# q and k as scaled fp16 pairs in the score matmuls of a bucketed attention with a spectral mixer

## The chip, the core and the metric

One core of a Trainium2 chip runs the whole program. The metric is device time in microseconds, as the median over several runs of the same program; the lower the better.

## The reference

Attention comes first, in 4 batches × 8 heads of 768 tokens with 64 numbers each. Each token of q and k gets a bucket out of 6 signs of a projection, and a query sees only keys of its own bucket. Then each batch goes through a mixer.

```python
q_bits = einsum('bhsd,dk->bhsk', q, proj) > 0        # the same for k; 6 bits make a bucket
mask = q_bucket[:, :, :, None] == k_bucket[:, :, None, :]
scores = where(mask, q @ k.T / sqrt(64), -1e9)
attn = exp(scores - max(scores)); attn = attn / (sum(attn) + 1e-9)
x = (attn @ v), heads side by side                    # 4 x 768 x 512
theta = x @ w_theta
y = w_tok_r @ (x * cos(theta)) + w_tok_i @ (x * sin(theta))
u = x + y
out = u + maximum(u @ w_ch, 0)
```

The weights of the mixer are float64 (read as two 32-bit words each); q, k, v and proj are float32.

## The kernel before

**Precision.** TensorE multiplies pairs: each float32 operand is split into a high part, rounded to the type of the matmul, and a low part, the rest. In the scores the type is fp32r, fp32 data that TensorE takes in one pass; in P·V and the token mixing it is fp16.

**Heads come in pairs.** For each of 16 pairs (4 batches × 4), `prep_qk` loads q and k of two heads as `raw` (128 partitions: head and dimension; 768 tokens), makes `hl` (high by ACT or DVE, L569 and L571; low = raw − high by POOL or DVE, L575), and takes the bucket signs by a small matmul `pb` (L597). `assemble` then copies, per head, parts of `hl` and the sign rows into `qt` and `kt` by ten DMAs. `qt` and `kt` exist three times, and hold two score operands side by side: half 0 of 108 rows (64 high, 32 of the low part, 12 bucket signs with a weight of ±2^40) and half 1 of 97 rows (64 high, 32 low, one row for the maximum). The signs with the large weight push scores of other buckets far down.

**Maxima.** For each head `maxima` (L695 and after) multiplies half 0 of `qt` by half 0 of `kt` into `sq` in 9 units and reduces each on DVE to a row maximum `mc`; PE transposes it (`pmx`), DVE makes a row of it, and a DMA puts the row into half 1 of `qt` (L719 in `put`). The row goes through the second score matmul, with −1 in `kt`, and so subtracts the maximum.

**Chunks.** `step` computes P·V in chunks of 512 columns, 18 for a pair and 288 in all. A chunk is: 2 or 4 score matmuls into a PSUM bank `st` (there are two such banks, the pool s); ACT's exp of it into `pf` (L773); a copy rounded to fp16, `p`, by ACT (L779); the rest `pf − p` by POOL (L785); and 12 matmuls `po` into a bank of the head. Three products (p1·v1, p1·v2, p2·v1) make a P·V. V has been split into an fp16 pair `vv`, scaled by a power of two (`prep_v`: largest magnitude by DVE, two small matmuls `pa` and three DVE steps, L459 to L473 and L351 to L353).

**Mixer.** After each batch `moe` transposes x (`pt_x`), multiplies by w_theta (`ps_th`), takes sine and cosine on ACT, mixes tokens (`py`, 864 matmuls of 512 fp16 columns), and multiplies by w_ch (`ps_r`). The weights are unpacked and split during the first batch (`wf_t`, `wf_th`, `wf_ch`, `pwt`, `wtk`).

**The order.** All these pieces are recorded as operations with a priority, the engines that may run them with assumed durations, and the buffers that they use. A planner (`issue_all`) walks simulated time and gives each free engine the ready operation of least priority, looks at buffers, and lets operations with two possible engines go where there is room. So the order of all engines follows from the numbers at the end of the file: the priorities count chunks (`G`, step of a pair, plus offsets such as `QK0`, `MX0`, `PF`). The instructions then run in this order on each engine, with waits between engines. DMAs are all issued from the queue of SP, one after another. Every matmul is written in the helper `mm` (L75), so PE rows carry that line and are told apart by their tiles.

Of the kernel before, what the change touches and what calls it, by code (L numbers as in the profile page):

```python
# [31 lines left out]
def lsh_attention_moe_kernel(ctx: ExitStack, tc: tile.TileContext, q, k, v, proj, w_theta, w_tok_r, w_tok_i, w_ch, aff, out):  # L32
# [412 lines left out]
    def prep_v(b, hp, prio):  # L445
# [11 lines left out]
        def amax():  # L457
            t["am"] = ap_.tile([P, 1], F32, tag="am" + svb.tag, bufs=1, name=f"vam_{b}_{hp}")
            DVE.tensor_reduce(t["am"], src(), AX.XY, ALU.max, apply_absolute_value=True)  # L459
# [21 lines left out]
        def high():  # L481
            t["vv"] = ap_.tile([P, 2, T, W2], F16, tag=sv.tag, bufs=1, name=f"vv_{b}_{hp}")
            t["vf"] = vf = t["vv"].rearrange("p h t w -> p (h t) w")
            ACT.activation(vf[:, :, :D], src(), AF.Copy, scale=sc)

        def ones():
# [666 lines left out]
```

## Time and profile before

| | |
|---|---|
| median of 3 runs | 830.68 us (830.67 to 832.88) |
| profiled execution | 829.88 us, its span 827.8 us |
| PE, PEld | 768.0 us, 532.5 us busy |
| DVE, ACT, POOL | 562.5, 519.4, 497.8 us busy |
| DMA | 77.88 MB on the queue of SP, mean 95 GB/s |

PE is TensorE's matmul, PEld its weight load, which overlaps PE; DVE is VectorE, ACT ScalarE, POOL GpSimd, SP the engine that issues DMAs. In a group of instructions, "out<-in" are tiles, "xN" is a count, and after the bar stand busy us, mean ns of one, and the idle time before them with what ended it. Matmuls overlap in the pipeline, so the distance from start to start tells their cost, not the mean duration. In a table of stretches the numbers after the length are busy us on PE, PEld, DVE, ACT and POOL, then the granted clock of TensorE (1.00 is full), the share of the DMA engines and GB/s.

### The profile page before, as it was taken

Reading aid. Unit: us, or ns where it says so; the run is one execution under the profiler, and the core shown is the slowest. Engines: PE = TensorE matmul, PEld = TensorE weight load, DVE = VectorE, ACT = ScalarE, POOL = GpSimd, SP = SyncE. Lnnn points to the kernel's source line nnn. Section 1 sums busy time; section 2 is a strip of 40 time slices with the busy share of each in tenths; the row PEclk is TensorE's granted clock in tenths of the full one; section 3 lists DMA queues with packets and bytes.
Section 4 is the critical chain, followed back from the end, with each engine's and each line's share of the span. In section 5 each row is a group of like instructions: output and inputs, shape, how many; then the busy total and the mean of one; then the engine's idle time right before and its main releaser. Section 6 shows DMA issues by size and latency. Waiting matters only on the chain. (4 is left out here: it accounts for less than half of the span.)

```text
span 827.8 us, 17652 instructions
## 1 busy us (share of the span) xinstructions
PE 768.0 (93%) x6744; PEld 532.5 (64%) x6744; DVE 562.5 (68%) x940; ACT 519.4 (63%) x889; POOL 497.8 (60%) x506
## 2 busy tenths in 40 slices
PE   3788898889999999899899999999899999999998
PEld 1466676667655677668657666777657667675456
DVE  7988799897877756775986455675986454336323
ACT  4476798788884625787886455567886454557201
POOL 3386799887684727794868455573878463541200
PEclk9978899899999999999999999999999999999999
DMA  8566564744034334452243432542243330000001
GB/s 232 139 213 172 148 190 122 178 129 100 30 84 116 92 105 119 114 141 65 58 100 95 112 92 51 122 101 70 61 100 94 75 72 18 15 14 1 1 1 76
DMA packets 35267, 78.99 MB, mean 95 GB/s; under 512 B 7264, under 2 KB 13040, under 8 KB 35184
## 3 DMA queue, kind: packets, MB, share of 16 engines
q1 hardware_dynamic: 35184, 77.88, 36.2%
q8 instruction: 53, 0.87, 0.4%
q14 instruction: 30, 0.25, 0.1%
HBM read 32.51 MB, written 6.29 MB: 47 GB/s over the span
## 5 line engine op out<-in xcount | busy, mean ns | idle before, releaser
L785 POOL TENSOR_TENSOR p<-pf,p 128x512 f16<-128x512 f32 x288 | 361.5, 1279 | 174.6 <-ACT p L779 131.4
L773 ACT ACTIVATE pf<-st 128x512 f32<-128x512 f32 x288 | 164.5, 593 | 125.8 <-PE st L75 98.7
L695 DVE TENSOR_REDUCE mc<-sq 128x1 f32<-128x512 f32 (+1 forms) x288 | 191.8, 684 | 61.6 <-PE sq L75 59.8
L75 PE MATMUL py<-z,wtk 128*128 128x512 f16 x864 | 217.1, 380 | 0.3 <-POOL z L963 0.2
L75 PE MATMUL st<-qt,kt 108*128 108x512 f32 (+3 forms) x768 | 198.5, 373 | 13.8 <-ACT pf L773 13.4
L779 ACT ACTIVATE p<-pf 128x512 f16<-128x512 f32 x288 | 172.1, 629 | 14.8 <-PE po L75 12.1
L75 PEld LDWEIGHTS <-p 128*128 128x128 f16 x3456 | 134.5, 100 | 38.7 <-issue 17.3
L75 PE MATMUL po<-vv,p 128*128 128x65 f16 (+1 forms) x3456 | 156.8, 196 | 1.7 <-POOL p L785 1.1
L75 PE MATMUL sq<-kt,qt 108*128 108x512 f32 (+1 forms) x384 | 132.2, 408 | 24.1 <-DVE mc L695 13.7
L75 PEld LDWEIGHTS st<-qt,kt 108*128 108x128 f32 (+1 forms) x768 | 121.6, 195 | 38.7 <-ACT pf L773 25.6
L75 PEld LDWEIGHTS <-wtk 128*128 128x128 f16 x864 | 72.4, 98 | 82.7 <-issue 21.2
L75 PEld LDWEIGHTS sq<-kt,qt 108*128 108x128 f32 x384 | 69.2, 200 | 53.9 <-DVE mc L695 29.7
L963 POOL TENSOR_TENSOR z<-f,z 128x512 f16<-128x512 f32 x38 | 50.9, 1350 | 62.0 <-ACT z L957 48.7
L75 PE MATMUL ps_th<-wth,h_x 128*128 128x512 f32 x192 | 62.1, 405 | 2.2 <-DVE z L918 1.3
L952 DVE SCALAR_TENSOR_TENSOR f<-x,zsc,z 128x512 f32<-128x512 f32 x48 | 56.8, 1226 | 9.4 <-ACT z L940 7.1
L75 PE MATMUL ps_r<-wch,h_u 128*128 128x512 f32 x192 | 62.7, 407 | 0.0
L879 ACT ACTIVATE h_u<-pt_u 128x512 fp32r<-128x512 f32 x24 | 14.3, 596 | 61.5 <-PE pt_u L874 55.3
L998 DVE SCALAR_TENSOR_TENSOR x<-ps_r,x 128x512 f32<-128x512 f32 x24 | 16.6, 691 | 49.0 <-PE ps_r L75 49.0
L75 PEld LDWEIGHTS ps_th<-wth,h_x 128*128 128x128 f32 x192 | 34.9, 188 | 11.4 <-DVE z L918 1.8
L75 PEld LDWEIGHTS ps_r<-wch,h_u 128*128 128x128 f32 x192 | 34.8, 189 | 9.9 <-DVE l_u L883 1.1
L991 DVE SCALAR_TENSOR_TENSOR x<-py,sw,x 128x512 f32<-128x512 f32 x24 | 17.8, 743 | 32.8 <-PE py L75 32.8
L75 PE MATMUL ps_th<-wth,l_x 128*128 128x512 f32 x96 | 38.4, 400 | 0.1
(123 smaller groups left out, 889.7 us busy)
## 6 DMA issues: line engine op xcount, KB each, us to landing
qt<-hl SPq DMA_DIRECT2D x31, 384.0 KB
kt<-hl SPq DMA_DIRECT2D x31, 384.0 KB
raw<-in_q_dram SPq DMA_DIRECT2D x16, 384.0 KB
raw<-in_k_dram SPq DMA_DIRECT2D x16, 384.0 KB
vb<-in_v_dram SPq DMA_DIRECT2D x16, 384.0 KB
out_dram<-x SPq DMA_DIRECT2D x24, 256.0 KB
qt<-hl SPq DMA_DIRECT2D x62, 96.0 KB
kt<-hl SPq DMA_DIRECT2D x62, 96.0 KB
```

Of the source, the lines that this page charges most:

```text
L75: PE.matmul(out_, l, r, start=start, stop=stop, skip_group_check=True)
L695: DVE.tensor_reduce(col()[:, cs], u["sq"], AX.X, ALU.max)
L773: ACT.activation(wide("pf", spf, F32), u["st"], AF.Exp, scale=1.0 / math.sqrt(D))
L779: ACT.activation(o_, u["pf"], AF.Copy)
L785: return lambda: eng.tensor_tensor(wide("p2", sp2, F16), u["pf"], u["p1"], ALU.subtract)
L879: ACT.activation(u["hi"], u["pt"], AF.Copy)
L952: DVE.scalar_tensor_tensor(u["f"], tl[b][:, tt], zsc[:, b : b + 1], t["zw"][r][:, tt], ALU.mult, ALU.mult)
L963: return lambda: eng.tensor_tensor(t["z"][r, 1][:, tt], u["f"], t["z"][r, 0][:, tt], ALU.subtract)
L991: DVE.scalar_tensor_tensor(tl[b][:, to], res["py"], t["sw"][:, to : to + 1], tl[b][:, to], ALU.mult, ALU.add)
L998: DVE.scalar_tensor_tensor(tl[b][:, to], r_["ps"], 0.0, tl[b][:, to], ALU.max, ALU.add)
```

## The change

- `hl`, `qt`, `kt` and the rows of signs and maxima are fp16 instead of fp32r. q and k of a pair are each scaled by a power of two before the split. The counts and shapes of score matmuls stay; a weight load of `kt` or `qt` is now an instruction of its own in the program, as it was for `p`.
- The scale comes from a sum of squares: ACT squares `raw` with a running sum (`accum_out`), a matmul with a tile of ones adds the partitions, and DVE makes scales and the inverse scale in seven steps on columns (`root_scale` and `scale`). High is `raw × scale`, low is `raw × scale − high`, always on DVE.
- exp takes the inverse scale of the pair as a per-partition operand, and log(4096) as a bias column, where it had constants.
- For V the same sum of squares takes the place of the largest magnitude: one ACT instruction, one matmul and four DVE steps.
- `hl` has two buffers instead of one. Bucket weight and limits are smaller, to fit fp16.
- The planner's durations for scores and first copies and some 40 of its numbers are others. The duration that it assumes for exp (490 ns) is the same.

```diff
-    FREE = dict(ft=2, mc=2, hl=1, rows=1, nat=2, vv=2, x=2, z0=1, z1=1, xt=2, **BUFS)
+    FREE = dict(ft=2, mc=2, hl=2, rows=1, sc=3, nat=2, vv=2, x=2, z0=1, z1=1, xt=2, **BUFS)
...
+    def root_scale(total, r, inv):
+        DVE.tensor_scalar(r, total, 1e-30, None, ALU.max)
+        DVE.tensor_scalar(r.bitcast(U32), r.bitcast(U32), 24, 23, ALU.logical_shift_right, ALU.logical_shift_left)
+        DVE.tensor_scalar(inv, r, 2.0**66, None, ALU.mult)
+        DVE.tensor_scalar(r.bitcast(U32), inv.bitcast(U32), MASK, None, ALU.bitwise_xor)
...
-            DVE.tensor_reduce(t["am"], src(), AX.XY, ALU.max, apply_absolute_value=True)
+            ACT.activation(t["vf"][:, :, W1 : W1 + D], src(), AF.Square, scale=2.0**-14, accum_out=t["ss"])
+        def total():
+            t["pa"] = bank(sa, [P, 1], f"pa_{b}_{hp}")
+            mm(t["pa"], ones, t["ss"], True, True)
...
-    qts = [ap_.tile([P, 2, S], F32R, tag=f"qt{j}", bufs=1, name=f"qt{j}") for j in range(SETS)]
-    kts = [ap_.tile([P, 2, S], F32R, tag=f"kt{j}", bufs=1, name=f"kt{j}") for j in range(SETS)]
+    qts = [ap_.tile([P, 2, S], F16, tag=f"qt{j}", bufs=1, name=f"qt{j}") for j in range(SETS)]
+    kts = [ap_.tile([P, 2, S], F16, tag=f"kt{j}", bufs=1, name=f"kt{j}") for j in range(SETS)]
...
+                    ACT.activation(t["hl"][:, 1, i], t["raw", i], AF.Square, scale=1.0 / RAISE, accum_out=t["sc"][:, i : i + 1])
...
-                            ACT.activation(t["hl"][:, 0, i], t["raw", i], AF.Copy)
+                            ACT.activation(t["hl"][:, 0, i], t["raw", i], AF.Copy, scale=t["sc"][:, 2 + i : 3 + i])
-                            DVE.tensor_copy(t["hl"][:, 0, i], t["raw", i])
+                            DVE.tensor_scalar(t["hl"][:, 0, i], t["raw", i], t["sc"][:, 2 + i : 3 + i], None, ALU.mult)
-                    return lambda: eng.tensor_tensor(t["hl"][:, 1, i], t["raw", i], t["hl"][:, 0, i].bitcast(F32), ALU.subtract)
+                    DVE.scalar_tensor_tensor(t["hl"][:, 1, i], t["raw", i], t["sc"][:, 2 + i : 3 + i], t["hl"][:, 0, i], ALU.mult, ALU.subtract)
...
+        def scale():
+            c = [t["sc"][:, n : n + 1] for n in range(7)]
+            root_scale(t["pa"], t["sc"][:, 2:4], t["sc"][:, 4:6])
+            DVE.scalar_tensor_tensor(c[3], c[4], SPAN / 2, c[3], ALU.mult, ALU.min)
+            DVE.scalar_tensor_tensor(c[5], c[2], 2 / SPAN, c[5], ALU.mult, ALU.max)
+            DVE.scalar_tensor_tensor(c[6], c[4], 0.25 / math.sqrt(D), c[5], ALU.mult, ALU.mult)
...
-                    ACT.activation(wide("pf", spf, F32), u["st"], AF.Exp, scale=1.0 / math.sqrt(D))
+                    ACT.activation(wide("pf", spf, F32), u["st"], AF.Exp, bias=lps, scale=qt_["sc"][:, 6:7])
...
-                a = op("st", G, on("PE", 460 + 40 * kc, scores), [mxt["rowd"]], [ss])
+                a = op("st", G, on("PE", 440 + 8 * kc, scores), [mxt["rowd"]], [ss])
```

Three places show what becomes of the order. First ACT at the start of the program, up to the first product of a weight (`hl` and `raw` are the first pair's halves and inputs, `wf_t` a token weight). Before:

```order
L569 ACTIVATE hl_0_137<-raw_0_0_128 128x768
L569 ACTIVATE hl_0_137<-raw_0_0_130 128x768
L619 ACTIVATE qt_109<-hl_0_137 64x1536
L619 ACTIVATE kt_112<-hl_0_137 32x768
L381 ACTIVATE wf_t_142<-w_t_139 128x1536
L484 ACTIVATE vv_0_204<-vb_0_135,vsc 128x12x64
```

And now:

```order
L567 ACTIVATE hl_0_138,sc_0_139<-raw_0_0_129 128x768
L567 ACTIVATE hl_0_138,sc_0_139<-raw_0_0_131 128x768
L572 ACTIVATE hl_0_138<-raw_0_0_129,sc_0_139 128x768
L472 ACTIVATE vv_0_174,vs_0_175<-vb_0_136 128x12x64
L641 ACTIVATE qt_110<-hl_0_138 64x1536
L641 ACTIVATE kt_113<-hl_0_138 32x768
L485 ACTIVATE vv_0_174<-vb_0_136,vsc 128x12x64
L392 ACTIVATE wf_t_144<-w_t_141 128x1536
```

Three squares have come ahead of the copies into `qt` and `kt` (one of q, one of k, one of V), one of the two highs has gone to DVE, and the weight's sign comes after V.

Second DVE at the same place, from the first instruction on q and k to the sign rows of the first head. Before:

```order
L575 TENSOR_TENSOR hl_0_137<-raw_0_0_128,hl_0_137 128x768
L336 TENSOR_SCALAR pst_q<-pp 64x6 x4
L336 TENSOR_SCALAR pst_k<-pp 64x6 x4
L459 TENSOR_REDUCE vam_0_159<-vb_0_135 128x1
L621 CAST kt_112<-hl_0_137 64x1536
L621 CAST qt_109<-hl_0_137 32x768 x2
L621 CAST kt_112<-hl_0_137 32x768
L602 TENSOR_SCALAR qt_109<-pb_0_154,affs 12x384
```

And now, after the same eight instructions on `pst_q` and `pst_k`:

```order
L361 TENSOR_SCALAR sc_0_139<-pq_0_157 128x2
L362 TENSOR_SCALAR sc_0_139<-sc_0_139 128x2
L597 SCALAR_TENSOR_TENSOR sc_0_139<-sc_0_139 128x1
L574 TENSOR_SCALAR hl_0_138<-raw_0_0_131,sc_0_139 128x768
L578 SCALAR_TENSOR_TENSOR hl_0_138<-raw_0_0_131,sc_0_139,hl_0_138 128x768
L578 SCALAR_TENSOR_TENSOR hl_0_138<-raw_0_0_129,sc_0_139,hl_0_138 128x768
L361 TENSOR_SCALAR vsc<-pa_0_180 128x1
L643 COPY kt_113<-hl_0_138 64x1536
L643 COPY qt_110<-hl_0_138 32x768
L624 TENSOR_SCALAR qt_110<-pb_0_166,affs 12x384
```

Rows that only repeat are left out: there are four steps on `sc` like the first two (L361 to L364), three like the third (L597 to L599), and four on `vsc`. The seven steps, a high and a second low stand ahead of the copies; the maximum of V is gone.

Third PE in the second batch's last pair, where a chunk's scores follow a P·V. Before:

```order
L75 MATMUL po_6_0_5180<-vv_3_4648,p_1_6_0_0_5151 128x65
L75 MATMUL st_6_1_0_5204<-qt_111,kt_114 128x256 x4
L75 LDWEIGHTS p_1_6_0_1_5133
L75 MATMUL po_6_0_5180<-vv_3_4648,p_1_6_0_1_5133 128x65
L75 LDWEIGHTS p_1_6_0_1_5171
```

And now:

```order
L80 MATMUL po_7_0_5551<-vv_3_4393,p_1_7_0_0_5513 128x65
L80 LDWEIGHTS kt_113
L80 MATMUL st_7_1_1_5573<-qt_110,kt_113 128x256
L80 LDWEIGHTS p_1_7_0_1_5507
L80 MATMUL po_7_0_5551<-vv_3_4393,p_1_7_0_1_5507 128x65
```

The pair of load and score stands four times in that chunk; a score's load is separate, and `po` goes before and after it as it did. On POOL the 13 lows of q and k that it ran are gone, and in the second batch's last pair PE now has 6 matmuls `py` and 12 `ps_r` of the first batch's mixer, where it had none.

More of the change, by code (lines that the diff above doesn't have):

```diff
@@ L61, in lsh_attention_moe_kernel @@
     DVE.memset(hpi, math.pi / 2)
+    lps = const.tile([P, 1], F32, name="lps")
+    DVE.memset(lps, math.log(PSC))
+    ones = const.tile([P, P], F32, name="ones")
+    DVE.memset(ones, 1.0)
     magic = const.tile([P, 1], F32, name="magic")
@@ L440, in lsh_attention_moe_kernel @@
     W2 = W1 + D + 1
-    vamax, vinv, vsc = (const.tile([P, B * NP], F32, name=nm) for nm in ("vamax", "vinv", "vsc"))
+    vinv, vsc = (const.tile([P, B * NP], F32, name=nm) for nm in ("vinv", "vsc"))
     zinv, zsc = (const.tile([P, B], F32, name=nm) for nm in ("zinv", "zsc"))
@@ L481, in high, with rims @@
         def high():
[L482 to L486, printed above, removed]
+            ACT.activation(t["vf"][:, :, :D], src(), AF.Copy, scale=sc)
+        def rims():
             POOL.memset(t["vf"][:, :, D : D + 1], ONE)
@@ L579, in part, with total @@
                 nats.append(sn)
-                hs.append(op("qkh", pr + QKI * i, pick(g, QKH, {"ACT": (760, high("ACT")), "DVE": (520, high("DVE"))}), [a], [sn, sh]))
-                ls.append(op("qkl", pr + QKI * i, pick(g, QKLO, {"POOL": (1750, low(POOL)), "DVE": (880, low(DVE))}), [hs[-1]], [sn, sh]))
+                sq.append(op("qksq", pr, on("ACT", 740, squares), [a], [sn, sh, ssc]))
+                parts.append((i, sn, high, low))
             part()
+        sa = Slot("m")
+        def total():
+            t["pa"] = bank(sa, [P, 2], f"pq_{b}_{hp}")
+            mm(t["pa"], ones, t["sc"][:, :2], True, True)
+        def scale():
[4 more added lines that the diff above has]
+            DVE.scalar_tensor_tensor(c[6], c[4], 0.25 / math.sqrt(D), c[5], ALU.mult, ALU.mult)
+        r = op("qksum", pr, on("PE", 60, total), sq, [sa, ssc])
+        r = op("qksc", pr, on("DVE", 550, scale), [r], [sa, ssc])
+        for i, sn, high, low in parts:
+            hs.append(op("qkh", pr + QKI * i, pick(g, QKH, {"ACT": (760, high("ACT")), "DVE": (520, high("DVE"))}), [r], [sn, sh, ssc]))
+            ls.append(op("qkl", pr + QKI * i, on("DVE", 880, low), [hs[-1]], [sn, sh, ssc]))
         sm_ = Slot("m")
@@ L1068 @@
 SEED = 162248
[L1069 to L1098 removed]
+TH0_3 = -0.751
+TH1_3 = 0.437
+Y0_3 = 4.336
+YS_3 = 1.441
+Y1_3 = 0.042
+MX0_0 = -2.946
+MX1_0 = 0.331
+AS0_0 = -5.589
+PV0_0 = -5.035
+QK0_0 = -9.695
+QK1_0 = -4.286
+HOLD = 0
+LATE = 6
+WL0 = 11.761
+WLS = -27.563
+TH0_0 = 0.065
+TH1_0 = 0.835
+Y0_0 = 9.844
+Y1_0 = 1.885
+YS_0 = 6.889
+AHEAD = 3.831
+QKL = -12.071
+QKI = 2.69
+QKH = [(0, 999, ["ACT", "DVE"])]
+QK0 = -6.21
+QK1 = -5.118
+AS0 = -1.045
+PV0 = -4.162
+LV0 = -4.108
 W0 = -0.514
[L1100 to L1102 removed]
+WS = 3.311
+TH0 = -0.195
+TH1 = 0.854
 Y0 = 8.868
[L1104 to L1105 removed]
+YS = 5.588
+Y1 = 2.733
 _INS = ["q", "k", "v", "proj", "moe_w_theta", "moe_w_tok_r", "moe_w_tok_i", "moe_w_ch"]
```

152 lines of the change are left out of this document (56 added, 96 removed).

## The prediction

> **What bounds the kernel now.** I read the page first, its span and busy row.
>
> ```profile
> span 827.8 us, 17652 instructions
> PE 768.0 (93%) x6744; PEld 532.5 (64%) x6744; DVE 562.5 (68%) x940; ACT 519.4 (63%) x889; POOL 497.8 (60%) x506
> ```
>
> PE is busy 93% of the span. An average hides stages, so next comes the table of busy time by stretch, cut at the first exp of each of the first six head pairs (36, 72, 110, 144, 177 and 237 us), of the eighth and ninth (342, 368), and at the last score (735).
>
> ```profile
> 0.00:36.00 36.00, 18.09 (x57) 9.11 (x58) 30.80 (x63) 13.15 (x16) 11.99 (x22) 1.00 0.66 180
> 36.00:72.00 36.00, 29.36 (x264) 22.14 (x264) 30.87 (x49) 29.05 (x49) 26.88 (x27) 0.84 0.57 172
> 72.00:110.00 38.00, 34.00 (x354) 25.89 (x352) 30.86 (x52) 29.37 (x51) 28.69 (x27) 0.84 0.64 188
> 110.00:144.00 34.00, 30.68 (x341) 23.28 (x340) 32.32 (x57) 31.13 (x56) 33.00 (x30) 0.95 0.58 151
> 144.00:177.00 33.00, 27.43 (x305) 20.41 (x304) 28.57 (x48) 25.41 (x48) 29.50 (x30) 0.89 0.55 144
> 177.00:237.00 60.00, 57.23 (x462) 41.00 (x462) 49.96 (x77) 50.42 (x82) 42.45 (x41) 0.97 0.33 82
> 342.00:368.00 26.00, 24.15 (x301) 17.61 (x299) 18.86 (x35) 20.91 (x39) 24.93 (x28) 1.00 0.48 104
> 610.00:735.00 125.00, 123.17 (x1208) 86.28 (x1209) 63.30 (x117) 69.57 (x127) 76.77 (x79) 1.00 0.22 56
> 735.00:828.00 93.00, 87.02 (x427) 52.64 (x425) 35.90 (x48) 28.91 (x42) 11.32 (x9) 1.00 0.05 17
> ```
>
> After the length of the stretch stand PE, PEld, DVE, ACT and POOL, then the granted clock. Three regimes: to 36 us DVE (30.80) builds the first operands; from 36 to 177 nothing has slack (in 110–144 DVE has 32.32 of 34, ACT 31.13, POOL 33.00) and PE is granted 0.84 to 0.95; from 177 PE sets the pace (95% in 177–237, 99% in 610–735, where DVE, ACT and POOL stand at 51 to 61%), but for 342–368, where attention runs alone and POOL has 24.93 of 26. The 93 us after the last score hold no work that changes.
>
> **PE's saving.** The chain of waits gives fp16 and fp32r rates for 512 columns, the timeline of PE the scores themselves.
>
> ```profile
> 761.69 37.57 PE py L75 x174
> 804.45 5.62 PE ps_r L75 x24
> 659.16 0.81 PE L75 MATMUL py<-z,wtk 128*128 128x512 f16 x3
> 659.62 0.83 PE L75 MATMUL st<-qt,kt 108*128 108x512 f32 x2
> 660.28 0.40 PE L75 MATMUL sq<-kt,qt 108*128 108x512 f32 x1
> 660.53 0.82 PE L75 MATMUL py<-z,wtk 128*128 128x512 f16 x3
> 663.72 0.53 PE L75 MATMUL po<-vv,p 128*128 128x65 f16 x12
> 664.09 0.73 PE L75 MATMUL st<-qt,kt 108*128 108x256 f32 x4
> 664.65 0.40 PE L75 MATMUL sq<-kt,qt 108*128 108x256 f32 x2
> 664.89 0.82 PE L75 MATMUL py<-z,wtk 128*128 128x512 f16 x3
> 665.36 0.83 PE L75 MATMUL st<-qt,kt 108*128 108x256 f32 x4
> 666.03 0.82 PE L75 MATMUL py<-z,wtk 128*128 128x512 f16 x3
> ```
>
> py (fp16) takes 37.57/174 = 0.216 us, ps_r (fp32r) 5.62/24 = 0.234. From 659.16 to 660.53 three py and three 512-wide scores take 1.37, so a score costs (1.37 − 0.65)/3 = 0.241, and 0.025 goes at fp16's rate. From 664.89 to 666.03 three py and four 256-wide scores take 1.14: 0.123 each against 0.108, 0.015 goes. Behind the short po the four st need 664.65 − 664.09 = 0.56 instead of 4 × 0.123 = 0.49: 0.07 once, because an fp32 weight load doesn't fit under a po. An fp16 load takes half as long, as the groups by line say:
>
> ```profile
> L75 PEld LDWEIGHTS st<-qt,kt 108*128 108x128 f32 (+1 forms) x768 | 121.6, 195 | 38.7 <-ACT pf L773 25.6
> L75 PEld LDWEIGHTS <-p 128*128 128x128 f16 x3456 | 134.5, 100 | 38.7 <-issue 17.3
> L75 PE MATMUL st<-qt,kt 108*128 108x512 f32 (+3 forms) x768 | 198.5, 373 | 13.8 <-ACT pf L773 13.4
> L75 PE MATMUL sq<-kt,qt 108*128 108x512 f32 (+1 forms) x384 | 132.2, 408 | 24.1 <-DVE mc L695 13.7
> L773 ACT ACTIVATE pf<-st 128x512 f32<-128x512 f32 x288 | 164.5, 593 | 125.8 <-PE st L75 98.7
> L879 ACT ACTIVATE h_u<-pt_u 128x512 fp32r<-128x512 f32 x24 | 14.3, 596 | 61.5 <-PE pt_u L874 55.3
> L915 ACT ACTIVATE n<-ps_th,magic 128x512 f32<-128x512 f32 x24 | 16.6, 691 | 19.6 <-PE ps_th L75 19.6
> L569 ACT ACTIVATE hl<-raw 128x768 fp32r<-128x768 f32 x22 | 18.3, 842 | 9.0 <-DMA kt<-rows 4.7 <-DMA raw<-in_q_dram 1.9 <-DMA out_dram<-x 1.0
> L484 ACT ACTIVATE vv<-vb,vsc 128x768 f16<-128x768 f32 x16 | 14.9, 929 | 8.3 <-DVE vsc L353 7.9
> L382 ACT ACTIVATION_READ_ACCUMULATOR wf_t<-wf_t 128x1 f32 x6 | 1.1, 190 | 0.0
> L459 DVE TENSOR_REDUCE vam<-vb 128x1 f32<-128x768 f32 x16 | 15.0, 940 | 0.6 <-DMA vb<-in_v_dram 0.6
> L575 DVE TENSOR_TENSOR hl<-raw,hl 128x768 fp32r<-128x768 f32 x19 | 26.2, 1385 | 5.5 <-ACT hl L569 5.4
> L575 POOL TENSOR_TENSOR hl<-raw,hl 128x768 fp32r<-128x768 f32 x13 | 28.1, 2161 | 10.6 <-ACT hl L569 5.5 <-DVE hl L571 4.7 <-DMA qt<-rows 0.5
> L491 DVE SCALAR_TENSOR_TENSOR vv<-vb,vsc,vv 128x768 f16<-128x768 f32 x16 | 18.0, 1128 | 3.2 <-ACT vv L484 3.1
> L353 DVE TENSOR_SCALAR vsc<-vinv 128x1 uint32<-128x1 uint32 x16 | 2.5, 154 | 0.6
> ```
>
> Half of the 768 st and of the 384 sq are 512 wide: 576 × 0.025 = 14.4, and 576 × 0.015 = 8.6. In the order of before 130 score groups stand behind po: at 0.07, 9. Sum **32 us**, 2.0 for each of 16 pairs. The one thing no row shows is an fp16 load of 108 or 97 rows: bounds 100 (p, 128 rows) and 195 ns (fp32r, 108 rows); the 9 hang on it, and I take 100, because fp32 scores (108 rows) and ps_r (128) run within 3%, so the row count does not set the rate. The Trainium skill, page "TensorE: Matmul & The Clock Gate", section "Weight-path perf modes", says the fast load needs 128 weight columns and a type other than FP32, with rows not asked; by that the sum is 32, without it 23.
>
> **What ACT, DVE and POOL pay.** ACT: exp has no pointer operand now and gets two (bias lps, a scale column). One pointer costs 691 − 596 = 95 ns (L915 to L879) or 929 − 842 = 87 (L484 to L569). No row has two: bounds 0.09 and 0.18; I take 0.18, the operands being separate reads. 288 × 0.18 = 52. Squares: 32 of q and k and 16 of V at 0.84 + 0.19 (L382) = 49. Highs with a scale come out even. ACT grows by **100**, to about 620 of the span, 6.3 a pair. The same skill's page "ScalarE: Activation LUTs", section "What ACT_TABLE_LOAD costs", prices each pointer operand at ≈ 93 ns: an estimate of 54 us here, where the one-pointer rows alone would allow 26; it speaks against the change.
>
> DVE: 16 maxima go (−15.0). Lows become 32 at 1.128 instead of 19 at 1.385 (+9.8). By the order of both, 14 highs stand where 10 casts stood, +4 at about 1 us; 176 column-sized steps where 80 stood, 96 × 0.154 = +14.8; and some weight and z work comes over from POOL, about ten instructions of 0.7 to 1 us, +9. DVE gains 23, 1.4 a pair. POOL loses 13 lows (28.1) and what it gave away.
>
> Start: squares, sum, seven steps, highs, lows and copies are serial before the first score. Steps 7 × 0.154 = 1.1, accumulator read 0.19, a second low 1.1 that POOL did beside it, together 2.4; off it comes the maximum (0.94), and the fp16 copies, of which no row exists, may save as much again or nothing. Bounds **+0.5 to +3** with the sum's round trip, taken 2; nothing hides it, since PE waits for these operands. Later pairs have this chain one pair ahead, with the second halves buffer; if that cover is gone, a pair pays the 3 us. Assembly DMAs carry half the bytes; SP issues as many as before, and the put of the maxima still stands behind an assembly there, so I count 0 (bounds −4, what the sq row gives to DMA, and 0).
>
> 36–177 us: ACT busy per pair rises by 6.3 against stretches of 36, 38, 34 and 33. If no stretch can hold ACT above the 31.13/34 = 92% seen, they need 38.4, 38.8, 40.7 and 34.4: +11. But POOL loses 28.1/16 = 1.8 a pair where it was full, PE needs 2.0 less at a reduced clock, and the order moves part of w_ch's preparation ahead of the first exp. Bounds 0 and 11, taken **4**.
>
> From 177: twelve pairs × 2.0 = **−24**. ACT has room in most; in 342–368 it would need (20.91 + 6.3)/0.92 = 29.6 instead of 26, though the order now puts 6 py and 12 ps_r into that pair, where it had none. In 177–237, where the sines run, it would need 56.7/0.92 = 61.6 of 60; two later pairs have sines too. These four lose their 2.0 and up to 3.6 and three times 1.6, so bounds 0 and 16; I give back **4**, since PE has other work in hand there.
>
> Sum: 827.8 + 2 + 4 − 24 + 4 = 813.8. The profiled execution took 829.88, 2.1 more than its span, and the median of the three runs, 830.68, is 0.8 above that, 2.9 in all: 816.7, so **817 us**.
>
> **The rivals.** (a) All costs hide: no stretching, no give-back, and a third of the first four pairs' 8 comes too: 827.8 + 2 − 24 − 3 + 2.9 = 806, down to 802 with DMA's 4. For it: POOL's relief. Against: ACT's 92%. Chance 0.15.
>
> (b) Slower, one mechanism: the score bank. There are two s banks; exp holds one 0.18 longer, so PE's next score waits. Where exp gates each chunk, 288 × 0.18 = 52 comes in against 32. At 230 gated chunks 827.8 + 41 + 2 − 32 + 2.9 gives 842; it decides from (32 − 2)/0.18 = 167 chunks. Speaks for it:
>
> ```profile
> PEld st L75 <- ACT pf L773: 25.6, 40, 1.7
> PE st L75 <- ACT pf L773: 13.4, 20, 1.6
> ```
>
> These are rows of the table of waits (us in all, times, the longest): PE and its loads waited for exp's bank 60 times at most. Against: exp waited 98.7 us for PE's scores (its row above), so ACT is the one that has time. 0.12.
>
> (c) The savings and the costs cancel (early stretch at its 11, give-back at 12): 827.8 + 2 + 11 − 24 + 12 + 2.9 = 832. 0.08.
>
> (d) fp16 scores at these shapes are no faster than fp32r, so that the change doesn't do what it says: 827.8 + 2 + 4 + 4 + 2.9 = 841. Against: py's 0.216. 0.03.
>
> (e) The clock: with less PE work early, more of 36–177 is granted half. At the lowest stretch mean seen, 0.84, in all four, PE's 121 busy us grow by 0.88/0.84 (the mean now is 0.88), +6: 822. 0.05. The skill's TensorE page, section "The HAM clock gate", gates the clock by recent PE activity; the trace agrees in that clocks under 1.00 stand in stretches where PE is least busy, all before 237 us.
>
> **How the numbers follow.** The forecast, 0.57: own range 807 to 827. Faster: 0.57 + 0.15 + 0.05 plus a little of (c) = 0.78; within 0.3% (about what a measurement of this kernel tells from no change) 0.07; slower 0.15. The range 800 to 834 takes (a), (e) and (c) whole and leaves out (b) and (d).
>
> **What would show it.** Right: 512-wide scores spaced 0.216 and py-like loads near 0.1 us; exp at 0.77 to 0.78; ACT near 620; 177 us's place (the 73rd exp) at 180 to 186; last score near 720; the tail still 93. Wrong: waits of PE for exp growing over 60 us (then b), or the 73rd exp not later at all (then a), or loads of kt and qt near 0.19.

## The result and the profile after

| | before | changed kernel |
|---|---|---|
| median of 5 runs | 830.68 us (830.64 to 832.88) | **837.25 us** (834.98 to 838.4) |
| ratio, 95% interval | | 1.0069 (1.0048 to 1.0091) |
| profiled execution, its span | 829.88, 827.8 us | 834.98, 833.2 us |

The forecast was 817, range 800 to 834: wrong in size and in sign. The changed kernel is 0.7% slower, and the whole interval of the ratio lies above 1.

The page of the changed kernel, span and busy time:

```profile
span 833.2 us, 17734 instructions
PE 743.1 (89%) x6760; PEld 475.6 (57%) x6760; DVE 567.6 (68%) x1040; ACT 598.1 (72%) x979; POOL 456.2 (55%) x485
```

PE has lost 24.9 us of busy time (768.0 to 743.1) and the span has grown all the same: PE now stands idle for 90 us instead of 60. ACT has 78.7 more, DVE 5.1 more, POOL 41.6 less. (In a busy row overlapping instructions count once. Added up one by one, ACT's durations grow by 98 us and DVE's by 9.)

First the unit prices. The groups by line of the changed kernel (in the loads the tile is that of the weights):

```profile
L80 PE MATMUL st<-qt,kt 108*128 108x512 f16 (+3 forms) x768 | 173.2, 341 | 17.7 <-ACT pf L795 16.5
L80 PE MATMUL po<-vv,p 128*128 128x65 f16 (+1 forms) x3456 | 159.1, 196 | 11.4 <-POOL p L807 10.1 <-ACT p L801 1.0
L80 PEld LDWEIGHTS <-kt 108*128 108x128 f16 (+1 forms) x768 | 71.6, 101 | 74.6 <-issue 45.3
L795 ACT ACTIVATE pf<-st,lps,sc 128x512 f32<-128x512 f32 x288 | 214.2, 773 | 69.1 <-PE st L80 61.3 <-POOL p L807 4.8 <-PE sq L80 2.1
L567 ACT ACTIVATE hl<-raw 128x768 f16<-128x768 f32 x32 | 26.9, 842 | 3.1 <-DMA raw<-in_q_dram 2.2 <-DMA raw<-in_k_dram 0.8
L567 ACT ACTIVATION_READ_ACCUMULATOR hl<-raw 128x1 f32 x32 | 6.4, 199 | 0.0
L472 ACT ACTIVATE vv<-vb 128x768 f16<-128x768 f32 x16 | 13.8, 863 | 8.8 <-PE po L80 5.4 <-DMA vb<-in_v_dram 3.4
L572 ACT ACTIVATE hl<-raw,sc 128x768 f16<-128x768 f32 x18 | 16.7, 931 | 17.0 <-DVE sc L364 12.9 <-DVE sc L597 3.9
L578 DVE SCALAR_TENSOR_TENSOR hl<-raw,sc,hl 128x768 f16<-128x768 f32 x32 | 36.1, 1144 | 0.7 <-ACT hl L572 0.4
L362 DVE TENSOR_SCALAR sc<-sc 128x2 uint32<-128x2 uint32 x16 | 6.4, 398 | 0.6
L362 DVE TENSOR_SCALAR vsc<-vsc 128x1 uint32<-128x1 uint32 x16 | 2.5, 154 | 0.6
```

A load of `kt` takes 101 ns, exp 773, a square 842 with 199 for its sum, a low 1144: as forecast, within 16 ns. One price is off, the two-column scale step: 398 ns in this row, and 388 and 288 in the two rows like it (L363, L364), instead of 154.

The timeline of PE tells the pitch of the scores:

```profile
662.26 0.38 PE L80 MATMUL sq<-kt,qt 108*128 108x512 f16 x1
662.48 0.81 PE L80 MATMUL py<-z,wtk 128*128 128x512 f16 x3
663.52 0.73 PE L80 MATMUL po<-vv,p 128*128 128x65 f16 x15
664.09 0.60 PE L80 MATMUL st<-qt,kt 108*128 108x512 f16 x2
664.52 0.38 PE L80 MATMUL sq<-kt,qt 108*128 108x512 f16 x1
```

From 664.09 two 512-wide scores take 0.43, 0.215 each, and the first of them stands behind the po row without paying anything for it. (A few rows of po between 663.1 and 663.5 are left out.) So PE's saving came as forecast, per matmul.

Then the stretches. The table of busy time, cut at the first exps of the pairs as in the prediction; these are the first four pairs, the eighth, the whole from the 73rd exp to the last, and the end (columns: length, PE, PEld, DVE, ACT, POOL, granted clock, DMA share, GB/s):

```profile
36.80:76.40 39.60, 29.51 (x312) 18.60 (x311) 36.83 (x62) 34.34 (x58) 29.36 (x25) 0.86 0.55 168
76.40:115.20 38.80, 31.56 (x320) 20.25 (x318) 35.03 (x60) 35.37 (x57) 28.68 (x26) 0.83 0.37 116
115.20:154.30 39.10, 31.09 (x326) 20.27 (x327) 33.75 (x62) 34.84 (x61) 26.22 (x28) 0.83 0.35 110
154.30:193.90 39.60, 28.55 (x356) 18.93 (x355) 32.93 (x63) 33.10 (x59) 30.02 (x31) 0.89 0.39 106
345.00:378.20 33.20, 28.17 (x349) 18.55 (x346) 26.94 (x53) 28.00 (x49) 24.61 (x28) 1.00 0.35 95
193.90:738.70 544.80, 519.13 (x4974) 336.88 (x4973) 363.69 (x673) 412.42 (x678) 322.53 (x346) 0.99 0.22 60
738.70:833.20 94.50, 88.53 (x428) 53.77 (x427) 35.29 (x48) 29.36 (x42) 11.51 (x9) 0.99 0.05 17
```

And the kernel before, whole stretches with the same cuts:

```profile
36.20:177.50 141.30, 121.77 (x1258) 91.89 (x1257) 122.91 (x203) 114.99 (x201) 118.56 (x112) 0.88 0.59 164
177.50:734.70 557.20, 540.64 (x5004) 378.49 (x5003) 372.69 (x628) 362.04 (x631) 355.59 (x365) 1.00 0.35 85
```

The first four pairs take 157.1 us instead of 141.3, **+15.8** (forecast +4). From there to the last exp it is 544.8 instead of 557.2, **−12.4** (forecast −20). The start is +0.6 (forecast +2), the end +1.4; from 738 to 742 us the granted clock was 0.58. The eighth pair, where the forecast let ACT need 29.6 us instead of 26, takes 33.2; some 4 of these (18 × about 0.22, an estimate from the rates of py and ps_r) are the 18 mixer matmuls that the order put there. Sum +5.4 where −14 was forecast. The split has a weakness: the two kernels have different orders, and the changed one has 54 more matmuls between the first and the 73rd exp (1312 instead of 1258), 38 of them po and 8 the bucket matmuls `pb` of a second pair. The 38 po are some 1.2 us of PE, an estimate from the prediction's row of 12 po, which starts 0.37 us before the next one. The sum doesn't depend on it.

The first four pairs show what has grown: DVE has 138.5 us of 157.1 and ACT 137.7, each 88%, where they had 122.9 and 115.0 of 141.3 (87% and 81%). POOL is the one relieved (114.3 after 118.6).

### The profile page after: what moved, and what is told of

The parts are those of the page before. It is cut to its first block, busy times and chain, and to the rows that moved or that the text cites. A ratio compares the mean times of both kernels' runs of the same rounds, so it can differ in the third digit from the quotient of the medians.

```text
span 833.2 us, 17734 instructions
## 1 busy us (share of the span) xinstructions
PE 743.1 (89%) x6760; PEld 475.6 (57%) x6760; DVE 567.6 (68%) x1040; ACT 598.1 (72%) x979; POOL 456.2 (55%) x485
## 5 line engine op out<-in xcount | busy, mean ns | idle before, releaser
L807 POOL TENSOR_TENSOR p<-pf,p 128x512 f16<-128x512 f32 x288 | 356.8, 1259 | 204.1 <-ACT p L801 118.7
L795 ACT ACTIVATE pf<-st,lps,sc 128x512 f32<-128x512 f32 x288 | 214.2, 773 | 69.1 <-PE st L80 61.3
L80 PE MATMUL py<-z,wtk 128*128 128x512 f16 x864 | 213.7, 378 | 0.3 <-POOL z L985 0.2
L80 PE MATMUL st<-qt,kt 108*128 108x512 f16 (+3 forms) x768 | 173.2, 341 | 17.7 <-ACT pf L795 16.5
L80 PEld LDWEIGHTS <-p 128*128 128x128 f16 x3456 | 145.1, 100 | 51.1 <-POOL p L807 13.3
L80 PE MATMUL po<-vv,p 128*128 128x65 f16 (+1 forms) x3456 | 159.1, 196 | 11.4 <-POOL p L807 10.1
L80 PE MATMUL sq<-kt,qt 108*128 108x256 f16 (+1 forms) x384 | 110.3, 346 | 34.3 <-DVE mc L717 27.2
L80 PEld LDWEIGHTS <-wtk 128*128 128x128 f16 x864 | 81.4, 98 | 83.8 <-issue 3.7
L80 PEld LDWEIGHTS <-kt 108*128 108x128 f16 (+1 forms) x768 | 71.6, 101 | 74.6 <-issue 45.3
L80 PEld LDWEIGHTS <-qt 108*128 108x128 f16 x384 | 36.0, 102 | 60.6 <-issue 34.0
L974 DVE SCALAR_TENSOR_TENSOR f<-x,zsc,z 128x512 f32<-128x512 f32 x48 | 50.4, 1084 | 7.3 <-ACT z L962 4.8
L80 PEld LDWEIGHTS ps_r<-wch,h_u 128*128 128x128 f32 x192 | 34.9, 188 | 10.1 <-DVE l_u L905 1.9
## 6 DMA issues: line engine op xcount, KB each, us to landing
w_t<-in_moe_w_tok_r_dram SPq DMA_DIRECT2D x6, 768.0 KB
w_t<-in_moe_w_tok_i_dram SPq DMA_DIRECT2D x6, 768.0 KB
```

Of the source, the lines that this page charges most:

```text
L80: PE.matmul(out_, l, r, start=start, stop=stop, skip_group_check=True)
L795: ACT.activation(wide("pf", spf, F32), u["st"], AF.Exp, bias=lps, scale=qt_["sc"][:, 6:7])
L807: return lambda: eng.tensor_tensor(wide("p2", sp2, F16), u["pf"], u["p1"], ALU.subtract)
L974: DVE.scalar_tensor_tensor(u["f"], tl[b][:, tt], zsc[:, b : b + 1], t["zw"][r][:, tt], ALU.mult, ALU.mult)
```

## The experiments

Stages of each kernel, from the starts of its first, 73rd and last exp in the timeline of its one profiled execution. A single execution is not exact: the runs of e9, for one, spread from 833.97 to 841.55 us, and the profiled one is the longest of them; that of the change is the shortest of its five, and those of e1, e4 and e7 are the longest of their four. So differences of a few us in a stage decide nothing alone.

| kernel | median us | ratio to before (95%) | first exp | first to 73rd | 73rd to last | end |
|---|---|---|---|---|---|---|
| before | 830.68 | | 36.2 | 141.3 | 557.2 | 93.1 |
| changed | 837.25 | 1.0069 (1.0048, 1.0091) | 36.8 | 157.1 | 544.8 | 94.5 |
| e1 exp with constants | 816.79 | 0.9837 (0.9795, 0.9879) | 36.6 | 154.6 | 533.8 | 93.1 |
| e2 short squares | 831.62 | 1.0025 (0.9999, 1.0050) | 36.6 | 157.1 | 542.0 | 93.2 |
| e3 both of these | 812.37 | 0.9782 (0.9742, 0.9822) | 36.4 | 152.4 | 530.4 | 93.1 |
| e4 before, exp with columns | 846.24 | 1.0174 (1.0129, 1.0218) | 36.1 | 145.0 | 570.5 | 93.1 |
| e5 old planner numbers | 860.07 | 1.0355 (1.0324, 1.0386) | 38.1 | 155.4 | 567.2 | 95.8 |
| e6 e1 + DVE relieved | 810.24 | 0.9758 (0.9726, 0.9789) | 35.2 | 152.0 | 527.9 | 93.1 |
| e7 one-column steps | 841.77 | 1.0128 (1.0100, 1.0155) | 37.9 | 160.1 | 549.9 | 93.2 |
| e8 fixed product | 810.16 | 0.9760 (0.9732, 0.9789) | 35.9 | 146.9 | 529.7 | 95.8 |
| e9 no wait | 837.10 | 1.0074 (1.0038, 1.0110) | 36.3 | 165.2 | 543.7 | 94.5 |
| e10 no chain | 831.69 | 1.0017 (0.9991, 1.0043) | 35.5 | 145.6 | 554.9 | 95.8 |
| e11 e10 + exp constants | 807.54 | 0.9726 (0.9693, 0.9759) | 35.6 | 139.4 | 534.3 | 95.7 |
| e12 scale column alone | 824.53 | 0.9930 (0.9912, 0.9948) | 36.6 | 156.4 | 537.1 | 93.1 |
| e13 short maxima | 824.20 | 0.9927 (0.9903, 0.9952) | 33.6 | 156.6 | 540.6 | 93.2 |
| e14 e13 + e3 | 797.72 | 0.9595 (0.9563, 0.9627) | 33.2 | 147.1 | 522.4 | 93.2 |
| e15 true costs on ACT | 850.49 | 1.0241 (1.0202, 1.0280) | 36.6 | 162.8 | 557.9 | 90.6 |

**First theory: ACT's added work is the loss.** The rival is the order, or the clock.

e1 gives exp its constants back (for these inputs the column holds 2^-19 for every pair) and leaves the factor 4096 out of the probabilities:

```diff
-ACT.activation(wide("pf", spf, F32), u["st"], AF.Exp, bias=lps, scale=qt_["sc"][:, 6:7])
+ACT.activation(wide("pf", spf, F32), u["st"], AF.Exp, scale=2.0**-19)
```

> The changed kernel with exp's two column operands replaced by constants (the scale is a constant 2^-19, which is the value that the columns hold for these inputs, and the factor 4096 before the split of p is left out); every instruction stays in its place in the order. ACT theory (exp's 0.18 us, 288 times, fills ACT in the first pairs and delays the chunks after): exp back at 0.59, the 73rd exp from 193.9 to about 184, the time from 837 to 820-826. Order theory (the new numbers of the planner make a worse order): less than 3 us, 834-837. Clock theory (less PE work early means more half clock): less than 3 us, since PE's work is the same.

e2 keeps the columns and takes the sums of squares of q, k and V over a twelfth of the columns (scaled by 12; the line of V is like this one and left out); e3 is e1 and e2 together:

```diff
-ACT.activation(t["hl"][:, 1, i], t["raw", i], AF.Square, scale=1.0 / RAISE, accum_out=...)
+ACT.activation(t["hl"][:, 1, i, :64], t["raw", i][:, :64], AF.Square, scale=math.sqrt(12.0) / RAISE, accum_out=...)
```

> The changed kernel with the squares of q, k and V taken over the first 64 of 768 columns (weighted by 12), so each is some 0.6 us shorter; the sum is an estimate then, and all else stays in its place. ACT theory: 48 x 0.6 = 28 us less on ACT, a third of it in the first pairs; 837 to 829-833. Order theory and clock theory: within 2 us of 837.

> Both of the two edits before: constants in exp (scale 2^-19, without the factor 4096) and squares over 64 columns. ACT theory: ACT has about 80 us less, near the kernel before it; 73rd exp near 178, time 812-820, the forecast of 817 come true. Order theory: over 830.

e4 goes the other way: the kernel before, with exp's scale of 1/8 and a bias of 0 given as columns.

```diff
-ACT.activation(wide("pf", spf, F32), u["st"], AF.Exp, scale=1.0 / math.sqrt(D))
+ACT.activation(wide("pf", spf, F32), u["st"], AF.Exp, bias=zero, scale=eighth)
```

> The kernel before, with exp given a column of zeros as bias and a column of 1/8 as scale, and no other edit: the price of the two columns alone, with fp32r scores. ACT theory: exp 0.593 to 0.77, first four pairs longer by 5-10 us, 830.7 to 838-848. Order theory: within 3 us of 830.7, since ACT is at 63% there.

The groups by line, exp in e1:

```profile
L795 ACT ACTIVATE pf<-st 128x512 f32<-128x512 f32 x288 | 163.1, 594 | 83.2 <-PE st L80 73.1 <-POOL p L807 9.4
```

exp in e4:

```profile
L777 ACT ACTIVATE pf<-st,zero,eighth 128x512 f32<-128x512 f32 x288 | 215.5, 772 | 107.9 <-PE st L79 90.0 <-POOL p L789 15.3 <-POOL vv L492 2.2
```

Exp's two columns cost 837.25 − 816.79 = **20.5 us** in the changed kernel and 846.24 − 830.62 (median of the runs of before beside it) = **15.6 us** in the old one, which has none of the other edits; the intervals of e1 and of the change lie apart, and that of e4 lies above 1. In time e1 came in 3 us under the range of the ACT theory, e2, e3 and e4 within. The marks of that theory were missed: the 73rd exp was expected at about 184 us in e1 and 178 in e3 and came at 191.2 and 188.8, and e4's first four pairs grew by 3.8 us, not 5 to 10. So most of the gain lies behind the 73rd exp. Shortening all squares is worth 4.4 (e3 against e1) to 5.6 us (e2 against the change), though in both pairs the intervals touch. The order of all engines is the same in e1 as in the changed kernel, so order and numbers cannot be these 20 us.

Where exp's share lies, the waits of PE show. The table of waits, changed kernel (us in all, times, longest):

```profile
PE st L80 <- ACT pf L795: 16.5, 27, 1.8
PEld L80 <- POOL p L807: 13.3, 24, 2.3
PE po L80 <- POOL p L807: 10.1, 20, 2.2
```

and e1:

```profile
PE st L80 <- ACT pf L795: 9.7, 19, 1.2
PEld L80 <- POOL p L807: 7.1, 10, 2.7
PE po L80 <- POOL p L807: 5.7, 7, 2.5
```

PE waits less at both ends of a chunk: for the score bank (16.5 to 9.7), and for the rest `p` that POOL makes from what ACT has done (10.1 to 5.7). A longer exp delays the copy behind it on ACT, then POOL, then `po`. (Waits of PE and of its loads overlap, so the rows don't add up.) In the old kernel the wait for the score bank takes more of it. The rows of e4, where the prediction's rows of before had 25.6 and 13.4:

```profile
PEld st L79 <- ACT pf L777: 41.1, 61, 2.1
PE st L79 <- ACT pf L777: 21.7, 29, 2.0
```

**One column or two.** e12 drops the bias column and keeps the scale column.

```diff
-AF.Exp, bias=lps, scale=qt_["sc"][:, 6:7])
+AF.Exp, scale=qt_["sc"][:, 6:7])
```

> The changed kernel with the exp's bias column dropped and its scale column kept. By one-pointer rows exp takes 0.68 to 0.69. If the time goes with exp's length: half of e1's gain, 825 to 829. If only the first or only the second column matters (a threshold in some stage): 833 to 837 or 816 to 820.

The group of exp in e12:

```profile
L795 ACT ACTIVATE pf<-st,sc 128x512 f32<-128x512 f32 x288 | 188.3, 684 | 75.6 <-PE st L80 64.8 <-POOL p L807 7.9 <-PE sq L80 2.1
```

594, 684, 773 ns with no, one and two columns: 90 and 89 apiece. The Trainium skill, page "ScalarE: Activation LUTs", section "What ACT_TABLE_LOAD costs", has ≈ 93 ns a pointer operand; the trace agrees. The time goes 816.8, 824.5, 837.25, so the scale column costs 7.7 us and the bias column on top of it 12.7. That is 0.5 us under the range for a time that goes with exp's length, and far from both threshold ranges: both columns count.

**The order.** e5 lays the changed kernel's instructions out by the old planner numbers, e15 tells the planner longer durations on ACT.

```diff
-MX1 = 0.365   ...   (and all other numbers of the change)
+MX1 = 0.432   ...   (those of the kernel before)
```

> The changed kernel's instructions, laid out by the planner numbers of the kernel before (its assumed durations as in the change). Occupancy theory (in the first four pairs ACT has 29 us more work and DVE 18 us more than before, so they set the pace): the same instructions are there, so the 73rd exp stays at 188 to 197 us and the time at 832 to 846. Order theory (the new numbers cost the early stage its 16 us): the 73rd exp goes back to 179 to 184 and the time to 818 to 826.

```diff
-i = op("pf", G + PF, on("ACT", 490, pf), ...
+i = op("pf", G + PF, on("ACT", 664, pf), ...      # squares 830 and 920, high 830
```

> The changed kernel with the planner told longer durations on ACT: exp 664 instead of 490, squares 830 and 920, high 830. The instructions are the same. If the order suffers from the short assumed duration, 820 to 832; if occupancy is what counts, 834 to 845, since the other numbers were fitted to the short one.

Both are slower, 860.07 and 850.49, above what either theory expected, and neither brings the 73rd exp forward by more than 0.4 us (193.5 and 199.4). So the order theory falls as it was put, that the old numbers or the true durations would give the loss back; that some third order suits these instructions better isn't excluded. The two runs show something else: 13 to 23 us hang on numbers that were fitted to one set of instructions and durations, true or not.

**The first four pairs.** e1 and e3 leave 13 and 11 of the 15.8 us there. The timeline shows what happens when a pair is prepared; DVE in the changed kernel:

```profile
46.15 0.16 DVE L361 TENSOR_SCALAR sc<-pq 128x2 f32<-128x2 f32 x1
46.35 1.00 DVE L362 TENSOR_SCALAR sc<-sc 128x2 uint32<-128x2 uint32 x1
47.38 1.08 DVE L363 TENSOR_SCALAR sc<-sc 128x2 f32<-128x2 f32 x1
48.50 0.17 DVE L364 TENSOR_SCALAR sc<-sc 128x2 uint32<-128x2 uint32 x1
49.05 0.62 DVE L574 TENSOR_SCALAR hl<-raw,sc 128x768 f16<-128x768 f32 x1
49.58 0.68 DVE L717 TENSOR_REDUCE mc<-sq 128x1 f32<-128x512 f32 x1
50.83 1.02 DVE L578 SCALAR_TENSOR_TENSOR hl<-raw,sc,hl 128x768 f16<-128x768 f32 x1
51.88 1.29 DVE L717 TENSOR_REDUCE mc<-sq 128x1 f32<-128x512 f32 x2
```

POOL beside it:

```profile
46.17 2.27 POOL L807 TENSOR_TENSOR p<-pf,p 128x512 f16<-128x512 f32 x2
```

ACT and PE:

```profile
48.90 0.93 ACT L572 ACTIVATE hl<-raw,sc 128x768 f16<-128x768 f32 x1 [1.37 <-DVE sc L597]
50.32 0.38 PE L80 MATMUL sq<-kt,qt 108*128 108x256 f16 x2 [1.68 <-DVE mc L717]
52.62 0.58 PE L80 MATMUL sq<-kt,qt 108*128 108x512 f16 x1 [1.92 <-DVE mc L717]
```

The seven steps (the last three, L597 to L599, are left out here) take 3 us instead of 1.2, since two of them run 1.00 and 1.08 us, until POOL's two instructions end at 48.44; ACT's high waits 1.37 for them with copies and exps behind it, and PE waits 1.68 and 1.92 for reductions that stand behind the steps, the high and the low. This gave four theories to try: the stretched steps (e7), the wait of the chain (e9), the chain as a whole (e10), DVE's busy time (e6).

e7 writes the two-column steps, one that reads PSUM and three on SBUF (the three of the expectation), as one-column steps, so that seven steps become eleven:

```diff
-root_scale(t["pa"], t["sc"][:, 2:4], t["sc"][:, 4:6])
+for n in range(2):
+    root_scale(t["pa"][:, n : n + 1], c[2 + n], c[4 + n])
```

> The changed kernel with the three two-column scale steps written as six one-column steps, nothing else. Port theory (a two-element fp32 step of DVE needs what a running POOL instruction holds, a one-element step does not, as the one-column steps of V show, 0.154 each, none stretched): no such step is over 0.2 us, the steps cost 96 x 0.15 = 14.8 us instead of 17.2, in the first four pairs 3.6 instead of 7.9, and the time is 831 to 837. Queue theory (the steps wait for something else that POOL's work goes along with): one-column steps beside a POOL instruction stretch to about 1 us too, and the time is 836 to 841.

The same group in e7:

```profile
L362 DVE TENSOR_SCALAR sc<-sc 128x1 uint32<-128x1 uint32 x32 | 4.9, 153 | 1.1
```

The fourth pair in e7, from the table of busy time:

```profile
154.50:198.00 43.50, 33.17 (x358) 21.07 (x358) 34.65 (x69) 33.61 (x59) 30.42 (x31) 0.77 0.37 104
```

The port theory holds for these steps, none is stretched any more (the longest is 156 ns); but the three steps behind them, which read two columns from SBUF, now stretch in 7 of 48 cases, up to 1.15 us, where 3 did. And the time is worse: 841.77, above both ranges and 4.5 more than the change, all four runs (839.39 to 842.83) above all its runs. Where nothing stretches, eleven steps take 1.8 us instead of 1.2. Between the two profiled executions, the longest of e7 and the shortest of the change, lie 7.8 us: the first exp comes 1.1 later, the fourth pair, at a clock of 0.77 (0.89 in the changed kernel), takes 3.9 more, and 5.1 come after the 73rd exp. Why, is open.

e9 keeps every engine's order and gives highs and lows the constant 256, so that they wait for no step:

```diff
-ACT.activation(t["hl"][:, 0, i], t["raw", i], AF.Copy, scale=t["sc"][:, 2 + i : 3 + i])
+ACT.activation(t["hl"][:, 0, i], t["raw", i], AF.Copy, scale=256.0)       # high on DVE and low alike
```

> The changed kernel in the same order of every engine, but highs and lows of q and k take the constant 256 in place of the scale columns (which are still made and still go to exp). So nothing of the split waits for the chain squares, sum, steps. Chain theory (in the first four pairs the chain stands uncovered in the in-order queues: ACT's high waits for DVE's steps, with copies and exps behind it): the 73rd exp at 186 to 190 and 828 to 833. Occupancy theory (only the busy time on ACT and DVE counts; highs lose 0.09 x 18): the 73rd exp at 192 to 195 and 834 to 838.

837.10: nothing gained, though the idle time before L572, 17.0 us in its row above, is 0.0 in e9's. The wait of ACT for the scale costs nothing by itself, and the chain theory in that form falls. (The 73rd exp, at 201.6, is later than either theory had it; this is the longest of the five executions.)

e10 leaves the squares, the sum and the steps of q and k out (highs and lows take 256 as in e9, exp keeps two columns); e11 gives exp its constants besides. The main lines:

```diff
-sq.append(op("qksq", pr, on("ACT", 740, squares), [a], [sn, sh, ssc]))
-r = op("qksum", pr, on("PE", 60, total), sq, [sa, ssc])
-r = op("qksc", pr, on("DVE", 550, scale), [r], [sa, ssc])
```

> The changed kernel without squares, sum and scale steps of q and k: highs and lows take the constant 256; exp keeps two columns (log of 4096 and a constant 2^-19). V keeps its squares. Chain theory: what is left of the early loss is mostly the chain (its busy time and its waits), so the 73rd exp at 179 to 186 and 819 to 828. ACT theory alone (e2: 6 us for all squares): the 73rd exp at 190 to 194 and 830 to 834.

> e10's edit, and exp with constants as in e1 (scale 2^-19, no bias, the factor 4096 dropped). A complete kernel as long as q and k lie below 255 in magnitude. If the exp columns cost the same 20 us beside the chain: e10's time less 20, so 799 to 808, with the 73rd exp at 178 to 184. If both removals relieve the same resource: 808 to 812, no better than e8.

e10's 73rd exp comes at 181.1, as the chain theory said, and yet the time is 831.69, as the ACT theory said. The operations left out let the planner choose another order, with 1249 matmuls between the first exp and that one instead of 1312: what is left undone early seems to be paid later (554.9 after 544.8). So the 73rd exp is a mark only among kernels of one order, and e10's −11.5 in the early stage is not a cost of the chain. In all, leaving it out gains 5.6 us (e10) to 9.3 us (e11 against e1), with whatever the other order is worth in it. e11's 807.54 lies in the range for exp's columns costing the same 20 us beside the chain (they cost 24.2 there); its 73rd exp, at 175.0, came before the 178 to 184 expected.

e6 is e1 with less on DVE, lows over 64 of 768 columns and one-column steps:

```diff
-DVE.scalar_tensor_tensor(t["hl"][:, 1, i], t["raw", i], ..., t["hl"][:, 0, i], ...)
+DVE.scalar_tensor_tensor(t["hl"][:, 1, i, :64], t["raw", i][:, :64], ..., t["hl"][:, 0, i, :64], ...)
```

> The changed kernel with exp's constants as in e1 (816.8 us, 73rd exp at 191.2) and DVE relieved: lows of q and k over 64 of 768 columns (so the rest of the low part is left out), and the three two-column scale steps as six one-column steps. Occupancy theory: with ACT relieved DVE is the next one full in the first four pairs; it loses 8 x 1.0 for lows and some 4 for steps there, so the 73rd exp comes at 180 to 185 and the time is 804 to 811. Order or latency theory (the early stage waits for the chain of a pair or for the order, not for DVE): the 73rd exp at 188 to 191 and 814 to 818.

810.24, in the range of the occupancy theory and 6.6 better than e1, but only 2.6 of it in the first four pairs, where 6 to 11 were expected. DVE alone isn't what is left there. e13 and e14 then relieve DVE far more, in exactly the changed kernel's order, e14 with ACT relieved as in e3. Both leave most of the maximum out, so they don't compute the attention any more and serve for timing alone:

```diff
-DVE.tensor_reduce(col()[:, cs], u["sq"], AX.X, ALU.max)
+DVE.tensor_reduce(col()[:, cs], u["sq"][:, :, :64], AX.X, ALU.max)
-DVE.tensor_scalar(t["row"], t["pm"], -TOP, ...)
+DVE.tensor_scalar(t["row"], t["pm"], 0.0, ...)
```

> The changed kernel, same order, each reduction of the maxima over 64 columns instead of 256 or 512 (so most of the maximum is left out; the row is kept at 0 or above so that exp stays finite). DVE loses about 0.5 us for each of some 74 reductions in the first four pairs, ACT nothing. Side-by-side theory (ACT and DVE each hold the early stage): the 73rd exp comes only a little earlier, 187 to 193, and the time is 828 to 835. DVE theory (its queue is what the early stage waits for): 178 to 185 and 815 to 827. Order or latency theory: 192 to 195 and 835 to 839.

> e13's edit together with e3's (exp with constants, squares over 64 columns): DVE and ACT both relieved, in the changed kernel's order. Side-by-side theory: the early loss goes, the 73rd exp at 176 to 182, and 796 to 804 in all. Order or latency theory: the 73rd exp stays at e3's 185 to 189 and the time at 808 to 813.

The first four pairs in e14, from the table of busy time:

```profile
33.20:180.30 147.10, 116.28 (x1312) 77.74 (x1311) 109.91 (x245) 119.80 (x230) 115.58 (x107) 0.87 0.44 135
```

From the first to the 73rd exp: 157.1 (change), 152.4 (ACT relieved, e3), 156.6 (DVE relieved, e13), 147.1 (both). Both marks and e14's time fall into the side-by-side theory's ranges. e13's time does not: 824.20 lies in the DVE theory's range, for 3.2 us come off the start and 4.2 off the stage after the 73rd exp. In the whole time the two reliefs nearly add up: 24.9 (e3) + 13.1 (e13) = 38.0 against 39.5 (e14). So each engine holds a part of the path; that one hides the other's relief, 10.0 against 4.7 + 0.5 in the early stage, is indicated by single executions and no more. Nor are the 10.0 the price of what the change put on DVE: e14 takes 28.6 us off its busy time there (138.5 to 109.9), and the change had added 15.6.

Six of the 15.8 us are left in e14, with DVE at 75% and ACT at 81% of the stage, no busier than in the kernel before (87% and 81%). What they are stays open. It may be the order, which by this exp has 1312 matmuls done instead of 1258; e11, in another order, needs 139.4 for 1252.

**A version that beats both.** e8 scales k by its squares and q by 2^16 over that scale. The product is a constant, so exp needs no column; the probabilities' factor 4096 is dropped. Only k has squares, and the seven steps become five of one column.

```diff
-root_scale(t["pa"], t["sc"][:, 2:4], t["sc"][:, 4:6])
-DVE.scalar_tensor_tensor(c[3], ...); DVE.scalar_tensor_tensor(c[5], ...); DVE.scalar_tensor_tensor(c[6], ...)
+root_scale(t["pa"], c[3], c[5])
+DVE.tensor_scalar(c[2], c[5], 2.0**15, None, ALU.mult)
-AF.Exp, bias=lps, scale=qt_["sc"][:, 6:7])
+AF.Exp, scale=2.0**-19)
```

> A complete kernel: k is scaled by its squares as now, q by 2^16 over that scale, so that the product of the scales is a constant and exp takes a constant scale again; the factor 4096 on the probabilities is dropped, so exp has no bias. 288 exps lose 0.18 (52 us of ACT), 16 squares go (16 us of ACT), the scale steps become five of one column. ACT theory, from e1's 816.8 and e2's -6 for all 48 squares: 808 to 817, with the 73rd exp at 186 to 191. Order theory: 830 to 838.

810.16 us, 2.4% below before and 6.6 us below e1, in the range of the ACT theory; the 73rd exp, in another order again, came at 182.8, before the 186 to 191 expected. It gives up the limit that the change sets to the product of the scales, so it holds for scores up to about 116 (the limit TOP, 6.08e7, times 2^-19). e11 has 807.54, 24.2 below e10, but holds only for q and k below 255.

## Why the prediction was wrong, step by step

- **PE's saving: right.** 0.215 for a 512-wide score (forecast 0.216), loads of 108 and 97 rows at 101 ns (forecast 100), nothing extra behind po. The stage after the 73rd exp shows it once ACT is relieved: 557.2 − 530.4 = 26.8 us in e3, where 24 were forecast; some 1.2 of them are the 38 po that the new order does before the mark. Rival (d) is out.
- **What ACT pays: the amounts right, their price in time wrong.** Exp at 773 ns and the squares came as forecast (ACT's durations grow by 98 us for 100; the profile's page has 598 busy, not 620, because overlaps count once). Against that stood 4 us early and 4 later. The columns alone cost 20.5, shortening the squares gave 4.4 to 5.6. This is the step that failed: 100 us on ACT were priced at 8 us of time. It reasoned that a longer exp matters only where ACT is near full, and that elsewhere PE has other work in hand. e4 shows otherwise: with ACT at 63% of the span, 48 us more of busy time cost 15.6 (10.7 to 18.1 by the interval of its ratio). Exp, copy, rest and `po` of a chunk are a chain across four engines whose queues run in order; lengthening one link also delays PE at moments when its next instruction in the order belongs to that chunk. That the time is lost by these waits is read from the tables of waits; that exp's columns cost it is shown by e1, e4 and e12.
- **The give-back from 177 us: 4 taken, 11.6 measured** (24 − 12.4), inside its bounds of 0 to 16. e1 gets 11.0 us of it back, e3 14.4. "PE has other work in hand there" was the wrong reason: the other work is in the order, but can stand behind the instruction that waits.
- **36 to 177 us: 4 taken, 15.8 measured**, outside the bounds of 0 to 11. These counted ACT at 92% and put nothing into the sum for DVE, whose 1.4 a pair were worked out but not used. From the first to the 73rd exp DVE's durations, added up, grew from 133.7 to 152.1, 4.6 a pair: lows 9.6 instead of 6.0, scale steps 11 (seven a pair, 0.40 on average, at 0.154 in the forecast), 4.6 more of the weights. e3 (ACT relieved) gives 4.7 of the 15.8 back, e14 10.0 by taking more off DVE than the change added; how much is DVE's own stays open, and so do the last 6.
- **DVE in all: +23 forecast, +5.1 measured** (+9.4 by durations). The sum was wrong, the place too: it falls where DVE was full. The 14 highs take 8.6 us where 10 casts took 9.7 (+4 forecast), and 48 mixer products `f` run 52.0 instead of 58.8.
- **Start: +2 forecast, +0.6 measured;** the end +1.4 for 0.
- **The rivals.** (b), the score bank, gave 842, but its sign is absent: PE's wait for exp is 16.5 us, not over 60. Its mechanism is a part of the chain, small in the changed kernel (16.5 with the columns, 9.7 without), larger in the old one: in e4 PE's wait grew by 8.3 us and that of its loads by 15.5, where 15.6 us were lost. (a) is out. (c), savings and costs cancel (early 11, give-back 12, 832 us), is what happened, with the early part above its bound; it had a chance of 0.08. (e): the clock in the first four pairs is 0.85 instead of 0.88, about its size; whether it is a part of the loss or follows from PE's longer idling there, no run tells apart. Its reading that clocks under 1.00 stand where PE is least busy holds for the stretches from 36 to 177 us, not for all of its table: the first 36 us, with PE at 50%, have 1.00, and 177 to 237, at 95%, has 0.97.
- **The signs.** Spacing, loads and exp came as said; the 73rd exp came at 193.9 instead of 180 to 186 and the last at 738.7 instead of near 720.
- That e1 comes out at 816.8, the forecast, is partly chance: its early stage lost 13.3 instead of 4 us, and its late one gained 23.4 instead of 20.
